# Block-layout key decays: sixteen small transfers replaced by four products with a spread identity

## The chip, the core and the metric

The kernel runs on one core of a Trainium2 chip. A core has a matrix engine (TensorE, "PE" in the profile, with its weight loads shown apart as "PEld"), three engines for elementwise work (VectorE "DVE", ScalarE "ACT", GpSimd "POOL") and a sync engine (SyncE "SP"), which here only issues transfers. A row such as "SPq" or "ACTq" stands for the transfer queue of that engine. Each engine works through its own instructions in program order and waits on semaphores for the others. The metric is device time in microseconds (us) of one execution, as a median over runs.

## The reference

Two blocks follow each other. The first is a recurrent retention: for each batch (4) and head (8), over 768 positions with head size 64,

```python
gamma = 1.0 - 2.0 ** (-5.0 - np.arange(H))
scale = 1.0 / np.sqrt(D)
for t in range(S):
    state = gamma * state + np.einsum('bhd,bhe->bhde', k[:, :, t], v[:, :, t])
    y[:, :, t] = scale * np.einsum('bhd,bhde->bhe', q[:, :, t], state)
```

The second takes y, laid out as 3072 tokens by 512 features, through a feed-forward layer:

```python
h = x @ w_in                      # 512 -> 2048
sp = np.maximum(h, 0.0) + np.log1p(np.exp(-np.abs(h)))
out = (h * erf(sp)) @ w_out       # 2048 -> 512
```

q, k and v arrive as float32, the two weight matrices as 64-bit floats, which the kernel turns into float32 on chip.

## The kernel before

**Work and its order.** The retention is done in chunks of 128 positions (24 chunks: batch b, chunk c of 6). In each chunk, keys and queries are scaled by powers of gamma, transposed, multiplied into scores, masked, and multiplied with the values; a state per head is carried from chunk to chunk. The order of the work is written out by hand: within each engine, instructions run in the order in which the Python code emits them (`manual_schedule`, line 173). Chunks 0 to 3 come first ("early", lines 1081 to 1123), while the weights are still being loaded and converted on VectorE; then the feed-forward layer of the first 512 tokens is woven with chunks 4 and 5 (lines 1151 to 1173), and from chunk 6 on both go on in steps of 256 tokens with a Strassen-like scheme of products until the end.

**Two layouts of the decays.** `decay_k` in device memory is [128 positions, 8 heads]. `d_k` (line 399) is a copy of it on chip, loaded at the outset by a transfer that ScalarE issues, and `d_s` (line 400) holds the decay of a whole chunk. From them VectorE and GpSimd make `kq_s` (lines 444 to 458), the scales for chunks whose positions lie on the partitions. Chunks from 6 on are loaded in another layout, in blocks: the 128 partitions are four groups of 32, where group 2s+d holds, for every odd or even head (s) and half of the head's features (d), 32 positions; there the scales are `kq_b` (line 462), with `by_b` (line 463) as the factor from one chunk to the next. `load_block_scales` (lines 465 to 473) fills the first slice of `kq_b` with 16 transfers of 512 bytes each (four partition groups times four head pairs, 128 elements of 4 bytes in each) and `by_b[:, 1]` with one more of 2 KB. They are issued by SP, in the middle of the kernel: the call stands at line 1170, in the third group of the first feed-forward part. `block_scales` (lines 475 to 483), called some groups later from the list at line 1147, makes all other slices from the first one; the readers are the multiplications at line 546 in `prepared`.

**The outset.** POOL makes an identity matrix `ident`. PE then runs `keep_warm(7)` (lines 493 to 497): seven products of `ident` with itself into a PSUM tile `o0` that nobody reads. Each float32 product of this kind is two PE instructions. Meanwhile the keys of chunk 0 land, VectorE multiplies them by `kq_s` (`K_`, line 514) and PE transposes them (`T`, line 524), ScalarE copies the result out of PSUM (line 530). Between the first transposes and scores, `keep_warm(2)`, `(1)` and `(2)` stand in the written order (lines 1084, 1087, 1093). `S_` are the scores (line 557), `M` the masks (line 569), `O_` the outputs (lines 597 to 618). The first use of the PSUM tile `o1` is in `O_(0)` (line 581).

**The weights.** `w_in_sb` has slots 0 to 25 in each of two halves; slots 16 to 23 serve first as room for raw weight pieces, slots 24 and 25 are first written by the sums of line 344, after 117 us. Raw pieces are loaded by SP (lines 264 and 272), each into room that the conversion of an earlier piece must have freed; chunks' k, q and v go through the same queue (lines 187, 205, 215).

## Time and profile before

| what | value |
|---|---|
| median of 3 runs | 662.81 us (662.61 to 662.85) |
| span of the profiled execution, first to last instruction | 660.9 us |
| PE busy | 655.7 us, 99%, 6200 instructions |
| PE weight loads busy | 557.3 us, 84% |
| DVE busy | 508.4 us, 77% |
| ACT busy | 280.2 us, 42% |
| POOL busy | 11.7 us, 2% |
| the 16 transfers into kq_b | issued from 88.4 to 97.1 us, 2.0 us to landing (median) |
| the transfer into by_b | issued at 97.2 us, 1.7 us to landing |

The profile is of one execution; no other time of that execution is given than its span, so the median stands 1.9 us above the span, and that distance is what lies around it. Rows of a timeline have the start in us, the duration in us (of several merged instructions, from the start of the first to the end of the last as far as the engine was busy), engine, line of the kernel, operation, output and inputs, shapes, count, and in brackets how long the engine had been idle before and what released it. Durations of matmuls are pipelined: one starts before the one before it has ended, so their pace is read from a series.

### The profile page before, as it was taken

What the parts mean: (1) busy time and instruction counts of PE and PEld (TensorE: products, weight loads), DVE (VectorE), ACT (ScalarE), POOL (GpSimd) and SP (SyncE); (2) the same over time, 40 slices, a digit from 0 to 9 for tenths busy, and PEclk for the clock granted to TensorE, in tenths of its full rate; (3) what the DMA queues carried; (4) which work ended last, traced back from release to release, by engine and by line L of the source; (5) the groups of instructions that cost most, each with busy time, mean ns of one, the idle gap of its engine ahead of it and who ended that gap; (6) DMA issues with size and microseconds to landing.
All of it is one profiled execution on the core that took longest, in us unless ns stands there. A gap on an engine that the chain in (4) does not pass through costs nothing.

```text
span 660.9 us, 15247 instructions
## 1 busy us (share of the span) xinstructions
PE 655.7 (99%) x6200; PEld 557.3 (84%) x6200; DVE 508.4 (77%) x1102; ACT 280.2 (42%) x402; POOL 11.7 (2%) x29
## 2 busy tenths in 40 slices
PE   8999999999999999999999999999999999999998
PEld 7744444576999999999999999999999999999997
DVE  5999999969986786788678678677687688476464
ACT  3468363445534334244254253342432542533440
POOL 1000000110100000000000000000000000000000
PEclk9999999999999999999999999999999999999999
DMA  9999844385753321222222322221231210000000
GB/s 188 223 264 231 211 129 107 63 152 90 144 123 61 85 47 32 67 47 46 70 44 47 73 39 46 42 72 37 44 79 36 46 53 1 2 34 0 1 33 32
DMA packets 159413, 51.88 MB, mean 78 GB/s; under 512 B 143216, under 2 KB 149744, under 8 KB 159344
## 3 DMA queue, kind: packets, MB, share of 16 engines
q1 hardware_dynamic: 157776, 46.72, 32.8%
q0 software_dynamic: 1152, 4.19, 3.4%
q8 instruction: 48, 0.79, 0.5%
q14 instruction: 21, 0.17, 0.1%
q10 hardware_dynamic: 416, 0.01, 0.0%
HBM read 40.39 MB, written 6.29 MB: 71 GB/s over the span
## 4 chain that ended last, share of the span: by engine, by line
PE 98%; DMA 1%; DVE 0%; ACT 0%; issue 0%
PE o L1034 37%; PE hp L951 22%; PE r L951 12%; PE hp L860 8%; PE o L896 8%; PE hp L980 2%; PE r L736 2%; PE hp L628 1%; PE o L772 1%; PE r L524 1%; PE r L557 1%; PE o L604 1%; PE r L751 1%; PE hp L751 1%; DMA kq<-in_k_dram 1%; PE r L772 0%
## 5 line engine op out<-in xcount | busy, mean ns | idle before, releaser
L1034 PE MATMUL o<-w_out_sb,h 128*128 128x256 f32 (+1 forms) x640 | 142.7, 380 | 0.0
L951 PE MATMUL hp<-xs,w_in_sb 128*128 128x128 f32 x988 | 138.1, 275 | 0.0
L1034 PEld LDWEIGHTS o<-w_out_sb,h 128*128 128x128 f32 x640 | 119.5, 190 | 16.6
L963 DVE TENSOR_TENSOR h<-h,hp 128x256 f32<-128x256 f32 x190 | 78.0, 418 | 70.5 <-PE hp L951 65.6
L951 PEld LDWEIGHTS hp<-xs,w_in_sb 128*128 128x128 f32 x988 | 128.4, 192 | 3.0
L1034 PE MATMUL o<-w_out_sb,e 128*128 128x256 f32 x480 | 113.5, 379 | 0.0
L1034 PEld LDWEIGHTS o<-w_out_sb,e 128*128 128x128 f32 x480 | 86.8, 190 | 9.4
L817 ACT ACTIVATE e<-h 128x2048 f32<-128x2048 f32 x22 | 42.1, 1912 | 119.6 <-DVE h L963 119.6
L963 DVE TENSOR_TENSOR h<-h,r 128x256 f32<-128x256 f32 x152 | 56.9, 415 | 22.3 <-PE r L951 21.4
L965 ACT COPY h<-hp 128x256 f32<-128x256 f32 x38 | 14.2, 373 | 130.7 <-PE hp L951 122.7
L951 PE MATMUL r<-xs,w_in_sb 128*128 128x128 f32 x456 | 63.3, 275 | 0.0
L951 PEld LDWEIGHTS r<-xs,w_in_sb 128*128 128x128 f32 x456 | 57.0, 192 | 0.0
L860 PE MATMUL hp<-xT,w_in_sb 128*128 128x512 f32 (+2 forms) x144 | 56.5, 548 | 0.0
L849 DVE TENSOR_TENSOR e<-h,e 128x1024 f32<-128x1024 f32 x42 | 49.2, 1213 | 8.0 <-ACT e L830 8.0
L860 PEld LDWEIGHTS hp<-xT,w_in_sb 128*128 128x128 f32 x144 | 25.8, 190 | 27.0 <-issue 24.6
L951 PE MATMUL hp<-xT,w_in_sb 128*128 128x128 f32 x304 | 46.3, 275 | 0.0
L951 PEld LDWEIGHTS hp<-xT,w_in_sb 128*128 128x128 f32 x304 | 41.5, 192 | 1.4 <-issue 0.5
L830 ACT ACTIVATE e<-e 128x2048 f32<-128x2048 f32 (+1 forms) x23 | 42.1, 1836 | 0.2
L967 ACT ACTIVATE h<-hp 128x256 f32<-128x256 f32 x57 | 21.9, 384 | 29.7 <-PE hp L951 28.3
L951 PE MATMUL r<-xT,w_in_sb 128*128 128x128 f32 x228 | 31.7, 275 | 0.0
L830 ACT ACT_TABLE_LOAD x24 | 30.8, 1283 | 0.4
L951 PEld LDWEIGHTS r<-xT,w_in_sb 128*128 128x128 f32 x228 | 28.5, 192 | 0.0
(164 smaller groups left out, 799.0 us busy)
## 6 DMA issues: line engine op xcount, KB each, us to landing
w_out_sb<-in_moe_w_out_dram SPq DMA_DIRECT2D x14, 512.0 KB, 5.2
kq<-in_k_dram SPq DMA_DIRECT2D x23, 256.0 KB, 4.0
v<-in_v_dram SPq DMA_DIRECT2D x23, 256.0 KB, 3.4
out_dram<-r SPq DMA_DIRECT2D x23, 256.0 KB, 2.9
kq<-in_q_dram SPq DMA_DIRECT2D x288, 16.0 KB, 1.9
kb<-in_k_dram SPq DMA_DIRECT2D x288, 16.0 KB, 1.8
w_in_sb<-in_moe_w_in_dram SPq DMA_DIRECT2D x8, 512.0 KB, 10.1
w_out_sb<-w_out_sb POOLq DMA_DIRECT2D x8, 512.0 KB, 5.3
```

The costliest lines, as they stand in the source:

```text
L736: nc.tensor.matmul(pp[r][col * D : (col + 1) * D, u % 2, t], x[own, u, :], QT[j][own, u, t], start=first(r, col), stop=True, skip_group_ch ...
L751: nc.tensor.matmul(other[a][own, u % 2, D:] if crossed else pp[a][own, u % 2, t], V[j][t, 2 * u + r, :], AM[j][t, r, u, :D], start=crossed ...
L817: nc.scalar.activation(E[g], HS[g], AF.Softplus)
L830: nc.scalar.activation(E[g][:, half], E[g][:, half], AF.Erf)
L849: nc.vector.tensor_tensor(E[g][:, half], HS[g][:, half], E[g][:, half], op=ALU.mult)
L860: nc.tensor.matmul(HP_[ft][:, t], w_in_of(ft, kk), XC[0][:, kk, t], start=(kk == 0), stop=(kk == n_k - 1),)
L896: nc.tensor.matmul(O[0][tt].rearrange("p (d c) -> p d c", d=2), E[g][:, u * TCH + tt * P : u * TCH + (tt + 1) * P], w_out_of(ft), start=(f ...
L951: nc.tensor.matmul(to[:, u, :], w_in_sb[:, s, w, u * P : (u + 1) * P], XS[m](x), start=first and u == 0, stop=True, skip_group_check=True,)
L963: nc.vector.tensor_tensor(h, h, of, op=ALU.add if plus else ALU.subtract)
L965: nc.scalar.copy(h, of)
L967: nc.scalar.activation(h, of, AF.Copy, scale=-1.0)
L1034: nc.tensor.matmul(O[m][i][:, half, at], G[g][a][:, u * P : (u + 1) * P], w_out_sb[:, s, OUT[b], u, at], start=i not in started, stop=(s = ...
```

## The change

Four things happen. A second use is made of slots 24 and 25 of `w_in_sb`: right after `load(0)` POOL fills them with `spread`, four matrices of 128x128, where matrix a repeats columns 32a to 32a+31 of the identity four times. `keep_warm(7)` becomes `keep_warm(5)`. After it, `spread_scales` multiplies each of the four matrices with `d_k` (8 columns) into a PSUM tile, so that each group of 32 partitions holds positions 32a to 32a+31; two ScalarE copies of 64 partitions by 16 elements pick the heads that belong to each half of the partitions into `kq_b`, and two POOL copies of 64 by 4 elements fill `by_b[:, 1]` from `d_s`. The function with the 17 transfers and its call go. `block_scales` stays where it was.

```diff
@@ -401,6 +401,11 @@
     load(0)
 
     nc.scalar.copy(idle_out, ident[:, :1])
+    spread = w_in_sb[:, 1, 24:26].rearrange("p x (b f) -> p (x b) f", f=P)
+    nc.gpsimd.tensor_copy(
+        spread.rearrange("p a (g f) -> p a g f", f=32),
+        ident.rearrange("p (a o f) -> p a o f", a=4, o=1).to_broadcast([P, 4, 4, 32]),
+    )
 
     for j in range(1, JPC):
         load(j)
@@ -462,15 +467,20 @@
     kq_b = const.tile([P, NC, 2, HP, 4], F32, name="kq_b")
     by_b = const.tile([P, 2, HP], F32, name="by_b")
 
-    def load_block_scales():
-        for s, d in itertools.product(range(2), range(2)):
-            part = slice((2 * s + d) * 32, (2 * s + d + 1) * 32)
-            for u in range(HP):
-                nc.sync.dma_start(
-                    kq_b[part, 0, 0, u],
-                    decay_k[:, 2 * u + s : 2 * u + s + 1].rearrange("(a p) h -> p (a h)", p=32),
-                )
-        nc.sync.dma_start(by_b[:, 1], decay_s)
+    def spread_scales():
+
+
+        for r in range(2):
+            own = slice(r * D, (r + 1) * D)
+            nc.gpsimd.tensor_copy(by_b[own, 1], d_s[own, r])
+        x = ps_o.tile([P, 4, H], F32, name="o1")
+        for a in range(4):
+            nc.tensor.matmul(x[:, a], spread[:, a], d_k, start=True, stop=True)
+        for r in range(2):
+            own = slice(r * D, (r + 1) * D)
+            nc.scalar.copy(
+                kq_b[own, 0, 0], x[own].rearrange("p a (u s) -> p s u a", s=2)[:, r]
+            )
@@ -494,7 +504,8 @@
-    keep_warm(7)
+    keep_warm(5)
+    spread_scales()
@@ -1167,7 +1178,6 @@
                 elif g == 2 and tt == 0:
                     sub_results(4)
                     sub_begin(5, ps_h)
-                    load_block_scales()
                     waiting.append((sub_states, 5))
```

## The prediction

> **What bounds the kernel now.** I read the page's busy shares first, then the waits of PE, then the timelines of the first 13 us, then SP's own timeline around the 16 transfers.

> ```profile
> span 660.9 us, 15247 instructions
> ...
> PE 655.7 (99%) x6200; PEld 557.3 (84%) x6200; DVE 508.4 (77%) x1102; ACT 280.2 (42%) x402; POOL 11.7 (2%) x29
> ...
> PE 98%; DMA 1%; DVE 0%; ACT 0%; issue 0%
> ```

> The reader is to see that PE is busy for all but 660.9 - 655.7 = 5.2 us, and that the chain of work that ended last is PE from end to end. The waits of PE, longest first, say where the engine stood still for another:

> ```profile
> PE o L495 <- POOL ident masks.py:199: 1.5, 1, 1.5
> PE o L597 <- DVE state L806: 0.3, 1, 0.3
> PE r L524 <- DVE kq L514: 0.3, 1, 0.3
> PE r L557 <- ACT qT L530: 0.2, 1, 0.2
> ```

> All four lie before 15 us (asked for the time from 17 us on, the same view is empty). So the end is set by two things only: how much PE has to do, and how its work begins. Nothing that happens to SP or DVE at 90 us is on the path unless it becomes so late that PE waits. The start, by the timelines of PE, of DVE and of ACT:

> ```profile
> 1.46 3.36 PE L495 MATMUL o<-ident 128*128 128x128 f32 x14 [1.46 <-POOL ident masks.py:199]
> 5.11 1.12 PE L524 MATMUL r<-ident,kq 128*128 128x128 f32 x4 [0.29 <-DVE kq L514]
> 6.02 1.06 PE L495 MATMUL o<-ident 128*128 128x128 f32 x4
> 6.87 0.68 PE L524 MATMUL hp<-ident,kq 128*128 128x128 f32 x4
> 7.39 0.39 PE L495 MATMUL o<-ident 128*128 128x128 f32 x2
> 7.72 0.66 PE L524 MATMUL r<-ident,kq 128*128 128x128 f32 x4
> ...
> 9.89 0.61 PE L495 MATMUL o<-ident 128*128 128x128 f32 x4
> ```

> ```profile
> 4.36 0.69 DVE L514 TENSOR_TENSOR kq<-kq,kq_s 128x512 f32<-128x512 f32 x1 [0.84 <-DMA kq<-in_k_dram]
> ```

> ```profile
> 6.26 0.59 ACT L530 COPY kT<-r 128x512 f32<-128x512 f32 x1 [3.02 <-PE r L524]
> ```

> The seven warm-up products are 14 instructions that end at 4.82. The first real work of PE starts at 5.11, released by DVE, which itself waited for the keys to land. The warm-up is therefore idle work, with 0.29 us of room behind it. Four transposes take 1.12 us at 5.11 and 0.66 us at 7.72: the pace of PE doubled in between. From 6.02, four warm-up instructions take 1.06, the last 0.42 of it (the line's median duration): (1.06 - 0.42) / 3 = 0.213 us apart. At 9.89 it is (0.61 - 0.275) / 3 = 0.112.

> **The change, part by part.**

> *Removed: 17 transfers at 88 us.* SP's timeline there:

> ```profile
> 88.36 8.74 SPq L469 DMA_DIRECT2D kq_b<-decay_k_dram  x16
> 97.15 0.43 SPq L473 DMA_DIRECT2D by_b<-decay_s_dram  x1
> 98.33 0.90 SPq L272 DMA_DIRECT2D w_out_sb<-in_moe_w_out_dram  x2
> ```

> They free 8.74 + 0.43 = 9.2 us of SP. But what comes next on SP, the weight piece at 98.33, did not follow at once: SP was free at 97.58 and stood 0.7 us for the conversion on DVE that frees the room. So the piece starts at 98.3 without the transfers too, and the chunk loads behind it, with it. SP's freed time becomes a longer wait; nothing comes earlier. Their readers, the three small steps of `block_scales` at 116.6, waited for nothing, and PE had all of its work. Gain: 0. From above, were the loads 9.2 us earlier, DVE's only wait for a load in that part (3.2 us, at 139.3, for chunk 7) would go; PE waits for nobody there, so 0 again.

> *Removed: two warm-up products,* 4 instructions of 0.213 = 0.85 us of PE, at the end of the row that starts at 1.46. The ten left take their turns up to 1.46 + 0.16 + 10 x 0.213 = 3.75 (0.16 is what the first, cold one took more).

> *Added on PE: four products with 8 columns,* 8 instructions, each with a full weight load of 128 columns. The trace has no such product. The nearest row is line 613, 64-column weights and 64 output columns: 16 in 0.63 us at the fast pace, 0.039 each. Twice the columns and half the pace make 0.16 each, 1.26 us in all. From below, 0.039 each, 0.3 us; from above, as long as a warm-up instruction, 0.213, 1.7 us. I take 1.26: the last starts by about 5.0, and the transposes, released at 5.11, are not held up. At 1.7 the last one ends its turn at 5.45, and the transposes come 0.34 us late; at 0.3, nothing changes. Two waits go with the products, and all of PE is queued behind them: `d_k`, there at 2.91 (DVE's first step, line 444, starts on it), and `spread`.

> *Added on POOL: the copy that makes `spread`,* 512 elements per partition. The rows: a memset of one element 0.10, of 128 elements 0.20; a copy of 64 elements 0.23. By the memset 0.10 + 512 x 0.0008 = 0.5 us, by the copy 0.10 + 512 x 0.0020 = 1.1 us. It starts when `ident` is done, about 1.5, and ends between 2.0 and 2.7; the products come at 3.75, so 1 us is spare. Queued behind it on POOL are the causal masks (ended at 2.49, now by 3.8; first read by DVE at 9.49), then the two new copies into `by_b`, 0.23 each, which wait for `d_s` (issued 1.27, landed 3.3 us later, 4.6), and then line 455 at 5.53. They end by 5.1; beside a DVE multiplication one of POOL's small steps took 0.71 in place of 0.20, so 5.6 at worst. Line 455 ended at 7.08 and is read by DVE at 8.86: 1.8 us of cover. Cost 0.

> *Added on ACT: two copies of 64x16.* Rows: one element 0.19, 256 elements 0.37. So 0.4 to 0.75 us between the products' end (5.2) and the copy at 6.26, which waits for PE anyway. ACT was idle for 3.02 us there. Cost 0; without that cover, up to 0.3 us. The PSUM tile is next wanted at 12.4.

> *Sum.* 0 for the transfers, 0 (0 to 0.34) for PE at the outset, 0 elsewhere: span 660.9, at most 661.3. The median stood 1.9 above the span, so **662.9** is the forecast, with 662.4 to 663.2 for this case.

> **The pace at the outset.** The row first: PE was busy from 1.46 and still slow at 6.87, though it had stood for only 0.29 us; the fast pace came at about 7.0. The granted clock in the windows view reads 1.00 throughout, so it doesn't show this; the spacing does. The products with 8 columns stream 8 columns where a warm-up instruction streams 128. If whatever sets the pace looks at streaming, PE looks idle from 3.75 to 5.11.

> [...]

> **The rivals.**

> *A. Nothing on the path moves* (above): 662.4 to 663.2.

> *B. The pace doubles later, slower than before.* Place: the transposes and scores from 7.06 on. In the trace, the chain up to the second query transposes has 3 + 2 + 4 + 8 = 17 steps (transposes, warm-up, transposes, pairs of scores) and those transposes start at 9.39. At the slow pace the 17 steps end at 7.06 + 17 x 0.213 = 10.7: 1.3 us late. ACT and PE hand over to each other there (the 0.2 in the waits of PE), so all of it reaches the end: 664.2. If the scores at 10.73 are slow as well, 8 steps of 0.10 to 0.11 more, 665.0. It decides once the doubling is later than about 7.7, since up to there PE waits for keys to land; a doubling at 8.5 costs some 0.4. For it: the streaming that goes. Against it: weight loads may count as work, and PE executes something nearly without a break.

> *C. Freed SP brings loads forward and PE gains.* Against it: SP waits for DVE at 98, and PE never waits after 17 us. It would need a wait that the profile doesn't show, 1.4 us or more: 661.4 or less.

> *D. The transfers' going shifts which earlier transfer a later one must wait for* (SP waited 1.0 and 0.9 us for earlier transfers around 100), and a weight piece comes late: PE would wait, 1.5 to 2 us, 664.5. Against it: DVE's conversions have no wait for pieces after 20 us, so a piece must be late by more than that unseen slack.

> **How the numbers follow.** A 0.50; B 0.36, with 0.17 of it beyond 0.2% (1.33 us, 664.14: about what a measurement of this kernel can tell from no change); C 0.05; D 0.05; other small things 0.04, half of them slower. Faster 0.05; slower 0.17 + 0.05 + 0.02 = 0.24; within 0.2% the rest, 0.71. The likeliest alone spans 662.4 to 663.2. The range reaches over most of B, up to 664.4, and leaves out the tail of B, C and most of D, under 2 in 10.

> **What would show it.** In the profile after: the eight instructions between about 3.75 and 5.1, first transposes at 5.1; transposes at 7.7 in 0.66 us (A) or about 1.1 (B); the scores' pairs 0.11 or 0.21 apart; SP idle from 88.4 to 98.3 with the piece still at 98.3 (if it comes sooner, my reading of that wait is wrong); no wait of PE after 17 us. The forecast fails if PE shows idle time or slow products that the trace of before has not, above all between 7 and 12 us.

## The result, and the profile after

| | before | after |
|---|---|---|
| median | 662.81 us (14 runs, 662.60 to 664.65) | 664.35 us (14 runs, 663.37 to 666.46) |
| ratio, 95% interval | | 1.0023 [1.0015, 1.0031] |
| span of the profiled execution | 660.9 us | 662.8 us |

The changed kernel is slower by 0.23%, 1.5 us. The forecast was 662.9, the case "nothing on the path moves". What happened is rival B, priced there at 664.2. Lines here are numbered by the changed kernel, some 11 higher than before: 505 is the warm-up, 478 the new products, 535 the transposes, 568 the scores. The page's first part and its chain:

```profile
span 662.8 us, 15243 instructions
...
PE 657.8 (99%) x6204; PEld 559.7 (84%) x6204; DVE 508.6 (77%) x1102; ACT 280.6 (42%) x404; POOL 12.9 (2%) x32
...
PE 99%; DVE 0%; ACT 0%; POOL 0%; issue 0%; POOLq 0%
```

PE is busy for 2.1 us longer (657.8 against 655.7), although 8 instructions replaced 4. The products alone can't be that: they take 1.71 us and the warm-up lost 0.85. PE's timeline of the outset shows where it comes from:

```profile
1.46 2.50 PE L505 MATMUL o<-ident 128*128 128x128 f32 x10 [1.46 <-POOL ident masks.py:199]
3.76 1.71 PE L478 MATMUL o<-d_k,w_in_sb 128*128 128x8 f32 x8
5.33 1.09 PE L535 MATMUL r<-ident,kq 128*128 128x128 f32 x4
6.21 1.06 PE L505 MATMUL o<-ident 128*128 128x128 f32 x4
7.07 1.06 PE L535 MATMUL hp<-ident,kq 128*128 128x128 f32 x4
7.92 0.63 PE L505 MATMUL o<-ident 128*128 128x128 f32 x2
8.35 1.06 PE L535 MATMUL r<-ident,kq 128*128 128x128 f32 x4
...
10.57 0.42 PE L568 MATMUL r<-qT,kT 64*128 64x128 f32 x1
...
10.78 0.33 PE L568 MATMUL r<-qT,kT 64*128 64x128 f32 x1
...
10.95 0.27 PE L568 MATMUL r<-qT,kT 64*128 64x128 f32 x1
...
11.16 0.66 PE L535 MATMUL hp<-ident,kq 128*128 128x128 f32 x4
```

Read the transposes first: four of them took 0.66 at 7.72 before, here they still take 1.06 at 8.35, and 0.66 only at 11.16. The score products fall from 0.42 to 0.27 around 10.9. That is when the pace doubled, 3.9 us later than the 7.0 of before. The second query transposes start at 11.16, where they started at 9.39: 1.77 us late. From there on the two traces run in step to the end, and 1.77 of the spans' difference of 1.9 is made in these 10 us. None of PE's waits for another engine has grown:

```profile
PE o L505 <- POOL ident masks.py:199: 1.5, 1, 1.5
PE o L608 <- DVE state L817: 0.3, 1, 0.3
PE r L568 <- ACT qT L541: 0.2, 1, 0.2
```

The wait of the first transposes for DVE is gone from the list. DVE's timeline shows that their data was there at 4.24 + 0.69 = 4.93; now PE was late, at 5.33:

```profile
4.24 0.69 DVE L525 TENSOR_TENSOR kq<-kq,kq_s 128x512 f32<-128x512 f32 x1 [0.60 <-DMA kq<-in_k_dram]
```

On POOL the copy that makes `spread` took 0.61 (bounds were 0.5 and 1.1) and the two copies into `by_b` 0.69, without delay for line 460:

```profile
1.47 0.61 POOL L405 COPY w_in_sb<-ident 128x512 f32<-128x512 f32 x1
...
4.52 0.69 POOL L475 COPY by_b<-d_s 64x4 f32<-64x4 f32 x2 [1.35 <-DMA d_s<-decay_s_dram]
5.41 1.60 POOL L460 TENSOR_TENSOR kq_s<-kq_s,by 128x8 f32<-128x8 f32 x4 [0.20 <-DVE kq_s L457]
```

And SP's timeline, where the 17 transfers are gone. The weight piece that started at 98.33 starts at 100.08, later by the same 1.75 us as everything on PE and DVE, although SP had nothing to do for 10 us. It waits for DVE, as the prediction had it (9.9 us in the list of SP's waits, for line 325):

```profile
89.20 0.88 SPq L272 DMA_DIRECT2D w_in_sb<-in_moe_w_out_dram  x2
100.08 1.24 SPq L272 DMA_DIRECT2D w_out_sb<-in_moe_w_out_dram  x2
```

### The profile page after: what moved, and what is told of

Read it like the earlier page. It is cut to its first block, busy times and chain, and to the rows that moved or that the text cites. A ratio compares the mean times of both kernels' runs of the same rounds, so it can differ in the third digit from the quotient of the medians.

```text
span 662.8 us, 15243 instructions
## 1 busy us (share of the span) xinstructions
PE 657.8 (99%) x6204; PEld 559.7 (84%) x6204; DVE 508.6 (77%) x1102; ACT 280.6 (42%) x404; POOL 12.9 (2%) x32
## 4 chain that ended last, share of the span: by engine, by line
PE 99%; DVE 0%; ACT 0%; POOL 0%; issue 0%; POOLq 0%
PE o L1045 37%; PE hp L962 22%; PE r L962 12%; PE hp L871 8%; PE o L907 8%; PE hp L991 2%; PE r L747 2%; PE hp L639 1%; PE o L783 1%; PE r L568 1%; PE r L535 1%; PE o L615 1%; PE r L762 1%; PE hp L762 1%; PE o L505 1%; PE r L783 0%
```

## The experiments

Theory G: the pace of PE doubles only after a stretch in which PE streams enough columns, and products of 8 columns are too little. Rivals: W, the time for which the products hold PE; T, the going of the transfers. Each kernel was timed in five rounds beside the kernel before; ratios are to it, and "before" is its median in the same runs.

| kernel | median | before | ratio, 95% interval | span of profile | pace doubles at |
|---|---|---|---|---|---|
| changed, again | 664.37 | 662.83 | 1.0023 [1.0014, 1.0032] | 662.5 | 10.3 |
| products stream 128 columns | 663.04 | 662.87 | 1.0000 [0.9992, 1.0009] | 661.3 | 7.4 |
| the same, warm-up of 4 | 663.06 | 662.83 | 1.0005 [0.9996, 1.0014] | 661.6 | 6.7 |
| transfers left out, nothing added | 663.01 | 662.87 | 1.0001 [0.9992, 1.0010] | 660.9 | 6.4 |
| products moved to the fast pace | 663.04 | 662.87 | 1.0002 [0.9993, 1.0012] | 661.0 | 5.3 |
| before, warm-up of 5 | 663.33 | 662.87 | 1.0009 [1.0001, 1.0018] | 661.4 | 8.1 |
| before, warm-up of 4 | 663.75 | 662.83 | 1.0014 [1.0005, 1.0023] | 661.9 | 9.5 |
| the same, again | 664.11 | 662.93 | 1.0016 [1.0007, 1.0025] | 662.2 | 9.3 |
| before, no first warm-up | 663.85 | 662.83 | 1.0013 [1.0004, 1.0022] | 662.1 | 9.6 |
| changed, warm-up of 4 | 664.62 | 662.76 | 1.0023 [1.0013, 1.0032] | 663.0 | 11.2 |
| changed, no first warm-up | 664.12 | 662.76 | 1.0017 [1.0008, 1.0025] | 662.5 | 10.2 |
| changed, warm-up of 4, ones for d_k | 664.07 | 662.77 | 1.0020 [1.0011, 1.0029] | 661.7 | 9.2 |

The last column is read from each profile's PE timeline, where the durations of one kind of product fall to the short ones. It belongs to the profiled execution, as the span does, and not to the median.

**Products that stream 128 columns.**

```diff
-        x = ps_o.tile([P, 4, H], F32, name="o1")
+        x = ps_o.tile([P, 4, 16, H], F32, name="o1")
-            nc.tensor.matmul(x[:, a], spread[:, a], d_k, start=True, stop=True)
+            nc.tensor.matmul(x[:, a], spread[:, a], d_k[:, None, :].to_broadcast([P, 16, H]), ...)
```

> The changed kernel with one edit: each of the four products streams d_k sixteen times over (128 columns in place of 8), so its 8 instructions keep the same weight loads and the same turns of 0.213 us and only stream more. Theory G (the pace doubles only after a stretch in which PE streams enough; the narrow products don't count): the doubling comes about as early as before the change, 662.8 to 663.2, and the widely spread times of the changed kernel close up. Rival W (the time that the products hold PE, with their weight loads and the late first transposes, is the cost, whatever they stream): as the changed kernel, 664.3. Rival T (the going of the transfers is the cost): 664.3 too.

Measured 663.04, spread from 662.89 to 663.80. The PE timeline of this kernel (line 507 warm-up, 537 transposes):

```profile
3.76 2.03 PE L478 MATMUL o<-d_k,w_in_sb 128*128 128x128 f32 x8
5.58 1.06 PE L537 MATMUL r<-ident,kq 128*128 128x128 f32 x4
6.43 1.06 PE L507 MATMUL o<-ident 128*128 128x128 f32 x4
7.28 0.66 PE L537 MATMUL hp<-ident,kq 128*128 128x128 f32 x4
```

The products hold PE longer than in the changed kernel, the first transposes come even later (5.58 against 5.33), and yet the second set already runs at 0.66. The eight weight loads are the same; streaming is the only thing added, and it takes the loss away. W and T both said 664.3; both fall as the main cause. The hold itself shows as 0.17, not clear of zero.

**The warm-up shortened, nothing added.**

```diff
-    keep_warm(7)
+    keep_warm(5)
```

> The kernel before with keep_warm(5) in place of keep_warm(7), nothing added; PE idles from about 3.8 us to the first transposes at 5.1. G: the same hole in the streaming as in the changed kernel without its products, so the pace doubles late in most executions: 663.6 to 664.4, with spread times. W: nothing is held up, 662.8. T: 662.8. If weight loads counted a little as work, this would be slower than the changed kernel less its 0.2 us of late transposes.

Measured 663.33 (663.04 to 664.33). Slower than before with nothing held up, so W and T fail here; but below the 663.6 that G named. In the timeline PE idles for 0.94 us in front of the transposes, and the pace doubles at 8.1, between the second warm-up (0.52 for two) and the third set of transposes:

```profile
4.91 1.12 PE L524 MATMUL r<-ident,kq 128*128 128x128 f32 x4 [0.94 <-DVE kq L514]
...
7.91 0.52 PE L495 MATMUL o<-ident 128*128 128x128 f32 x2
8.27 0.60 PE L524 MATMUL r<-ident,kq 128*128 128x128 f32 x4
```

**The transfers left out, nothing added.** kq_b and by_b are filled with ones, so the blocks' scales are not computed.

```diff
-                    load_block_scales()
...
     keep_warm(7)
+    nc.gpsimd.memset(kq_b[:, 0, 0], 1.0)
+    nc.gpsimd.memset(by_b[:, 1], 1.0)
```

> The kernel before with the 17 transfers left out and kq_b and by_b filled with ones by two memsets at the outset, so the scales of the blocks from chunk 6 on are not computed. It is the change's removal alone. G and W: 662.8, the weight piece still starts at 98.3. T: 664 or more, or, if freed SP helps, below 662.5.

Measured 663.01, 1.0001 [0.9992, 1.0010]. Leaving the 17 transfers out changed nothing clear of the noise, neither way; the weight piece starts at 98.53, against 98.33. T is out.

**The products at the fast pace.**

```diff
-    keep_warm(5)
-    spread_scales()
+    keep_warm(7)
...
     T(1, 1)
-    keep_warm(2)
+    spread_scales()
```

> The changed kernel with keep_warm(7) back at the outset and the four products moved to where keep_warm(2) stood after the second chunk's-first query transposes (T(1, 1)), in place of those two warm-up products. There PE already runs at the fast pace: 8 instructions of 0.112 = 0.9 us in place of 4, into a wait of PE for ScalarE that had 0.3 us left, so some 0.1 to 0.2 us late. G: 662.8 to 663.1. W: the products cost their time wherever they stand, less at the fast pace: 663.0 to 663.3. T: 664.3.

Measured 663.04, which lies in the ranges of G and of W, so this run does not decide between them; T's 664.3 it excludes. Its timeline:

```profile
5.05 0.77 PE L534 MATMUL r<-ident,kq 128*128 128x128 f32 x4 [0.24 <-DVE kq L524]
...
9.88 0.96 PE L478 MATMUL o<-d_k,w_in_sb 128*128 128x8 f32 x8
10.76 0.37 PE L567 MATMUL r<-qT,kT 64*128 64x128 f32 x1
```

The same 8 instructions take 0.96 here, and the scores that started at 10.73 before start at 10.76. So the function of the change can be had for nothing, but no faster than before: here the products fill the time in which PE stood for ScalarE (0.23 us before, no wait here). The pace doubled at 5.3 in this execution, during the first transposes (0.77), and the span is still 661.0: this earlier doubling gains nothing, since the next set of transposes waits for DVE and its keys anyway (PE stood 0.69 us for them).

**The changed kernel again.** No edit.

> The changed kernel unaltered, on the chip and beside the runs that the next three are compared with. [...]

Measured 664.37 (663.56 to 665.00), doubling at 10.3. The median comes back, and the place of the doubling is another one, 10.3 against the 10.9 of the first profile.

**A shorter and no first warm-up, nothing added.**

```diff
-    keep_warm(7)
+    keep_warm(4)    # the other kernel: keep_warm(0)
```

In the second of the texts, N is the reading that narrow products do harm of their own, and G2 the reading that they don't; both are set out with the kernels of narrow products below.

> The kernel before with keep_warm(4), nothing added: the last warm-up instruction takes its turn at 3.3 and PE idles for 1.6 us, which is as long as the changed kernel streams next to nothing (3.76 to 5.33), where keep_warm(5) left 1.15 us and cost 0.46. G, with the length of the hole as the size that counts: 663.8 to 664.2, nearly the changed kernel. If the narrow products do harm of their own beyond the hole: 663.3 to 663.6, like keep_warm(5). W: 662.8.

> The kernel before with keep_warm(4) once more, on the chip and beside the runs of the kernel above. G2 and N: 663.5 to 664.0, as before; G2 has the two within 0.3 of each other.

> The kernel before without the first warm-up, keep_warm(0): PE first streams at 4.9 to 5.1. [...] W: 662.8, since the products that go are read by nobody.

Measured 663.75 and 664.11 for keep_warm(4) in two sets of runs, 663.85 for none. 663.75 lies just below G's range and above the 663.3 to 663.6 of the other reading; 664.11 lies above its 663.5 to 664.0, and the two sets of one kernel differ by 0.36, not by 0.3 or less. That is how well these spread times are known. From the first set's profile, with PE idle before the transposes and the pace doubling at the scores:

```profile
5.02 1.11 PE L524 MATMUL r<-ident,kq 128*128 128x128 f32 x4 [1.49 <-DVE kq L514]
...
9.20 0.48 PE L557 MATMUL r<-qT,kT 64*128 64x128 f32 x1
...
9.52 0.27 PE L557 MATMUL r<-qT,kT 64*128 64x128 f32 x1
```

With no warm-up at all the loss is 1.0 us, and four products before a hole of 1.5 us are as good as none. The changed kernel, with a warm-up of five, loses 1.5: more than with no warm-up.

**Wide products after a warm-up of 4.**

```diff
-    keep_warm(5)    # of the kernel with products of 128 columns
+    keep_warm(4)
```

> The changed kernel with the wide products of the first experiment and keep_warm(4) in place of 5, so that PE is done with them about 0.43 us earlier and the first transposes are no longer held up. G: 662.7 to 663.0, no better than before, since up to 7.7 us PE waits for the keys in any case. W: 0.2 to 0.4 below the first experiment.

Measured 663.06, just above G's range. Its transposes start at 5.04 in place of 5.58, and the median is no lower than the 663.04 of the first experiment, where W asked for 0.2 to 0.4 less. The medians alone are weak evidence here, since the profile of this kernel has a wait at 54 us that the others lack (last section); but the shortest spans of the two kernels' runs are equal, too, 660.9.

**Narrow products that come earlier.** The loss beyond "no warm-up" was still open.

```diff
-    keep_warm(5)    # of the changed kernel
+    keep_warm(4)    # the other kernel: keep_warm(0)
```

> The changed kernel with keep_warm(4) in place of 5 and nothing else: the narrow products end 0.43 us earlier, so the first transposes start at 4.9 to 5.0, when their data is there, in place of 5.33. The kernels without products and with less warm-up cost 0.9 to 1.0 (four and no warm-up products), the changed kernel 1.5. G with a second part, G2 (the late doubling costs up to 1.0, and the 0.4 us by which the products hold up the transposes is paid in full, since at the slow pace nothing hides it): 663.7 to 664.0, faster than the changed kernel although it warms up less. Rival N (narrow products harm by themselves, for instance by keeping the pace down longer than an idle PE does): 664.3 or more. W: 663.9, too, but close together.

> The changed kernel with keep_warm(0): PE's first work are the narrow products, from about 3.0 (when d_k has landed) to 4.7, then the transposes as soon as their data is there. G2: as the kernel before without its first warm-up, 663.7 to 664.0. N: 664.3 or more. If weight loads with next to no streaming count as work for the pace: clearly below that kernel, 663.2 to 663.5.

Measured 664.62 and 664.12. Both missed G2's ranges: the first lies where N had it (664.3 or more), the second between the two. The timeline of the first shows that the edit did not do what it was for:

```profile
1.46 2.07 PE L505 MATMUL o<-ident 128*128 128x128 f32 x8 [1.46 <-POOL ident masks.py:199]
3.77 1.84 PE L478 MATMUL o<-d_k,w_in_sb 128*128 128x8 f32 x8 [0.23 <-DMA d_k<-decay_k_dram]
5.46 1.09 PE L535 MATMUL r<-ident,kq 128*128 128x128 f32 x4
```

`d_k` landed only at about 3.65 in this execution (2.91 in the first profile), the products waited for it, and the transposes came no earlier than in the changed kernel. The kernel without warm-up is 0.27 above its counterpart without products, and not at the 663.2 to 663.5 that it was to have if weight loads counted as work. But it, too, waited for `d_k`: its products start at 3.74 and its transposes at 5.44, against 4.86 without products. So neither kernel tells N and G2 apart.

**Narrow products that wait for no transfer.** Ones stand in for d_k, so the blocks' scales are wrong.

```diff
+    ones = const.tile([P, H], F32, name="ones")
+    nc.gpsimd.memset(ones, 1.0)
...
-            nc.tensor.matmul(x[:, a], spread[:, a], d_k, start=True, stop=True)
+            nc.tensor.matmul(x[:, a], spread[:, a], ones, start=True, stop=True)
...
-    keep_warm(5)
+    keep_warm(4)
```

> As the kernel with narrow products after keep_warm(4), but the products take 8 columns of ones, set by one small memset, in place of d_k, so kq_b holds no decays and the scales of the blocks are wrong. In that kernel's profile d_k landed only at 3.65 us, so the products ended at 5.46 and the transposes were held up after all; here no transfer is waited for, the products run from 3.33 to 5.04, and the transposes start at 4.9 to 5.1. The same warm-up without products gave 663.75 and 664.11 in two sets of runs. G2 (the products cost by holding the transposes up, and by streaming nothing): 663.6 to 664.2, like those. N (narrow products harm by themselves): 664.5 or more.

Measured 664.07, within G2's range. The timeline:

```profile
3.33 1.71 PE L480 MATMUL o<-ones,w_in_sb 128*128 128x8 f32 x8
4.90 1.09 PE L537 MATMUL r<-ident,kq 128*128 128x128 f32 x4
...
7.92 1.06 PE L537 MATMUL r<-ident,kq 128*128 128x128 f32 x4
...
9.26 0.27 PE L570 MATMUL r<-qT,kT 64*128 64x128 f32 x1
```

The transposes are not held up, PE works through 8 full weight loads in place of idling, and the time is that of keep_warm(4) with an idle PE, within what these runs can tell: 1.30 above the kernel before, against 0.92 and 1.18. The spans of the runs are closer still, with medians of 662.0 here and 662.0 and 662.3 there. This profile is also the clearest sign that weight loads did not count as work here: PE executes without a break from 1.46 on, and the pace doubles only at 9.2, while in the profiles of the kernel before and of both kernels with wide products it had doubled by 7.4. So in these runs narrow products were worth to the pace what idling was worth (664.07 against 663.75 and 664.11), and did no harm of their own that can be seen.

## Why the prediction was right in its range and wrong in its choice

*Bound and removed work: right.* PE's work and its outset set the end (the first 1% of the chain is the load of the keys, so it is not PE quite from end to end). The transfers were worth nothing that can be measured (1.0001), SP's freed time became waiting, nothing came earlier. Rivals C and D did not happen.

*POOL and ACT: right in that all is covered.* The copy took 0.61 (forecast 0.5 to 1.1), `by_b` 0.69 (forecast twice 0.23), ScalarE's two copies 0.34 (forecast 0.4 to 0.75).

*The eight instructions: wrong size.* "I take 1.26 ... the transposes, released at 5.11, are not held up." They took 1.71, the upper end; all but the first are 0.213 apart, a full turn each, with 8 columns as with 128. The row of line 613, 64-column weights in pairs, was no guide to a full weight load. The transposes started at 5.33, with data ready at 4.93, 0.4 us late. With early doubling that is nearly hidden (the wide products, later still, show 0.17); that it is paid in full at the slow pace is likely, but no run shows it by itself.

*The choice between A and B: the step that failed.* The prediction saw that streaming goes, and gave A 0.50 against 0.36 for B, since "weight loads may count as work, and PE executes something nearly without a break". The runs showed the opposite: eight weight loads counted like idling (664.07 with ones for d_k, against 663.75 and 664.11 with keep_warm(4)), and 128 streamed columns behind the same weight loads took the whole loss away (664.37 to 663.04, where before is 662.87).

*B's price: right mechanism, somewhat small.* It was 1.3 us, from 17 steps all at the slow pace, with the late transposes left out. That the doubling would come no earlier than their end at 10.7 was the author's estimate, and no row of before shows it; the profile of the changed kernel has it at 10.9. The profile shows 0.22 late at the first transposes and 1.77 at the end of the 17 steps. Across profiles, once the doubling is later than 8, the span goes with its place: from 8.1 and 661.4 to 11.2 and 663.0 in the table, (663.0 - 661.4) / (11.2 - 8.1) = 0.5 us for each us. That agrees with the turns: what takes 1 us at 0.213 a turn takes 0.53 at 0.112. The others lie within 0.3 of that line: the second run of keep_warm(4) some 0.2 above it (DVE released its second transposes 0.58 us late), the first 0.2 and the one with ones for d_k 0.3 below. The prediction let the cost begin at 7.7; the same line reaches the 660.9 of before near 7.1. That the changed kernel's runs spread over 3 us (their spans from 661.6 to 663.4, the rest lies around the spans) where most of those before lie within 0.5 was not in the forecast's numbers. It fits a place of the doubling that varies from execution to execution, as the two profiles of this kernel have it (10.9 and 10.3); the other runs' places are not known.

*Open.* How the 1.5 us divides: 0.9 to 1.2 for the hole alone, 1.3 with narrow products that hold nothing up, 1.5 with the hold, and 1.9 in the kernel with a warm-up of four whose products waited for `d_k`. The steps between are of the size by which two sets of one kernel differ, so the order is plausible and the parts are not measured. Nor was any number of columns between 8 and 128 tried, and how much streaming the doubling needs, over what time, is not shown: the profiles say only where it fell, from 5.3 to 11.2.

## What to carry to other kernels

Don't take a warm-up for idle work that may be swapped for any work of the same PE time: what brought the fast pace in these runs was streamed columns (664.37 with 8 of them in each product, 663.04 with 128), so replace it by products that stream as much, for instance by broadcasting the moving operand, or put narrow products where the pace is already fast (663.04 there, too). Price the two instructions of a narrow float32 product with 128-column weights by turns, not by columns: here all but the first were 0.213 us apart at the slow pace, as the warm-up instructions were, and eight took (10.76 - 9.88) / 8 = 0.11 each at the fast one. And before counting on freed transfer slots, look at what the next transfer on that queue waits for.

## What the runs showed of the hardware

```profile
40.49 6.81 DMA w_out_sb<-in_moe_w_out_dram
...
53.46 0.49 ACT qT L543
53.96 0.04 issue
54.00 0.69 PE r L641 x32
```
